# The expert's tokens gathered in quarter rows and turned on VectorE instead of TensorE

## The chip, the cores and the metric

The kernel runs on one core of a Trainium2 chip. The metric is the device time of one execution in microseconds (us), as a median of several runs. The engines are TensorE (PE in the profile, its weight loads PEld), VectorE (DVE), ScalarE (ACT), GpSimd (POOL) and SyncE (SP, which only issues transfers here). SBUF is the memory on the core in which the tiles lie, PSUM the one into which TensorE writes, DRAM the chip's large memory.

## The reference, cut to what matters

```python
# attention: B=8, H=8, S=576, D=64, causal, window 128, a linear bias by distance
x = attention(q, k, v)                      # [4608, 512]
logits = x @ w_gate                         # [4608, 8]
# greedy: the largest logit first; a token goes to one expert, an expert takes 576 tokens
for idx in np.argsort(-logits.flatten()):
    tok, e = idx // 8, idx % 8
    if assigned[tok] >= 0 or counts[e] >= 576: continue
    assigned[tok] = e; counts[e] += 1
for e in range(8):
    mask = assigned == e
    out[mask] = np.maximum(x[mask] @ w1[e], 0) @ w2[e]     # w1 512x1024, w2 1024x512
```

## The kernel before

**Stages.** Attention comes first (to about 220 us of the profile). It writes x to DRAM. Then the router makes the token list of the first expert (to about 242 us), and the rest is eight experts, one after the other, here k = 0 to 7 in the order in which they fill up.

**One expert.** Each fp32 operand of the two layers is split into two parts (`hh`/`xh` the rounded one, `hlo`/`xl` the rest; `hl` holds both parts of a weight), and a product is three matmuls. `layer1` runs over eight blocks f of 128 hidden units: 24 matmuls of 288 tokens each (`ph`, L893). Each f fills two PSUM banks and there are four, so f+2 can begin only when ScalarE (L899) and VectorE (L904) have read the banks of f. `layer2` runs over five tiles t of tokens (four of 128, one of 64, whose two halves are added by L932 and L933), 112 matmuls in all (`po`, L922, L923, L925). After each tile a scatter (an indirect DMA issued by POOL, L934) writes its rows to the places in the output that the list gives; the fifth of expert k is sent when layer 1 of k+1 has already begun.

**Beside the matmuls.** Both layers hand control back often (31 times per expert), and `slot(k, i)` then issues what else there is to do: one step of the router, one weight load (SP) or one split of a loaded weight (`split`: ScalarE's copy and VectorE's two subtractions `hl`, L837). A scheduler then puts the instructions of each engine into a row, and the engine works through this row in order; an instruction whose data isn't there holds up all behind it on its engine. Instructions marked with `keep_in_program_order` keep the order of the code among themselves. Before the change, transfers of the expert stage are not marked.

**The tokens of the next expert.** From step 16 of expert k on, `slot` gathers the tokens of k+1 (`gather`, five indirect DMAs on POOL, L846, each for up to 128 rows of 2 KB, one token per partition) and `turn` brings the 512 features to the partitions: per tile four transposes on TensorE (L870, into the bank `pg`), ScalarE's copy to `xh` (L873), VectorE's subtraction to `xl` (L874). `xh` and `xl` exist once, so their parts for k+1 can be written only when layer 1 of k has read them.

**The router.** `route` (the generator `Router.phase`) makes one list in about 15 steps; `WAITS` says how many slots lie between them. From k=1 on it works one expert further ahead, so that during expert k the list of k+2 is made. The steps touched here: `place` and `indicate` (`kq`, `ind`, L545, L555), `count` (nine matmuls, L579), `enough` (`odd`, `junk`, `sat`, L587 to L593, on VectorE, and a small matmul of `sat`, L596, whose result `narrow` uses for a new bound `lo`, L646); then the update of the table L1 of logits on POOL (L764, L759, L765), from which the next list begins; and from each chosen token's rank the list itself: the rank is divided by 64 slots, one-hot tables `loOH` (L736), `hOH` and `mv` are made on VectorE, and 18 matmuls of 40 columns (L741) turn them into `idx`, 128 partitions by five tiles. Constants come with one DMA at the start (`craw`).

```python
WAITS = (2, 1, 3, 1, 1, 2, 3)
...
        if i >= 16 and k + 1 in r.idx:
            if k not in gathers:
                gathers[k], st["turn"] = m.turn(m.gather(r.idx[k + 1])), i + TURN_WAIT
            elif i >= st["turn"]:
                next(gathers[k], None)
```

## Time and profile before

| | us |
|---|---|
| median of 3 runs | 715.52 (715.28 to 719.58) |
| the profiled execution, its own time | 715.13 |
| its span in the profile | 713.4 |
| attention | to about 220 |
| eight experts | about 242 to 713 |
| one expert in the steady part | 58 |
| PE / DVE / ACT / POOL busy over the span | 679.1 / 466.0 / 331.1 / 154.5 |

The page of a profile gives the busy time of each engine, the span in 40 slices (a digit is the busy share in tenths; `PEclk` is the clock that TensorE was granted), the groups of instructions by line, and the chain of waits that ended last. A row of the timeline has start, duration, engine, line, operation, output and input, and in square brackets how long the engine was idle before and what ended that. A row of the windows has busy time of each engine, with the count of instructions, then TensorE's clock, the share of the DMA engines and GB/s. The profiled execution took 1.7 us more than its span.

### The profile page before, as it was taken

The numbers are of one execution on the slowest core, as the hardware profiler recorded it, in microseconds if no ns is written. First come the engines' busy times: TensorE is split into PE (matmuls) and PEld (weight loads), VectorE is DVE, ScalarE is ACT, GpSimd is POOL, SyncE is SP. The second block draws the span as 40 slices with busy tenths as digits, with TensorE's granted clock in tenths as the row PEclk, the third lists the DMA queues.
The fourth block names the chain that finished last, engine by engine and source line by source line (L and its number), as shares of the span: only waits on it lengthen the run. The fifth ranks groups of instructions, "written<-read, shape, count | busy, mean of one in ns | idle before, by whom it ended". The sixth has DMA issues, their size and how long they took to land.

```text
span 713.4 us, 19210 instructions
## 1 busy us (share of the span) xinstructions
PE 679.1 (95%) x7447; PEld 596.6 (84%) x7447; DVE 466.0 (65%) x1855; ACT 331.1 (46%) x991; POOL 154.5 (22%) x337
## 2 busy tenths in 40 slices
PE   7999999999995699999999999999999999999996
PEld 4898888888874399789889889988988988988985
DVE  6778777877887789869578828846765724523210
ACT  6888888888873253324233223314324324322210
POOL 4121221221220301533042132132033023011011
PEclk9999999999997699999999999999999999999998
DMA  8465465465522352718135235135134334301001
GB/s 301 137 212 181 145 215 181 154 211 177 163 85 61 115 190 89 238 44 272 47 122 205 84 109 177 47 117 177 60 119 131 122 104 137 131 30 37 1 24 49
DMA packets 35140, 92.74 MB, mean 130 GB/s; under 512 B 3808, under 2 KB 13152, under 8 KB 35040
## 3 DMA queue, kind: packets, MB, share of 16 engines
q1 hardware_dynamic: 29152, 72.55, 31.0%
q0 software_dynamic: 5888, 18.88, 8.1%
q8 instruction: 61, 1.00, 0.6%
q14 instruction: 39, 0.32, 0.1%
HBM read 72.54 MB, written 18.87 MB: 128 GB/s over the span
## 4 chain that ended last, share of the span: by engine, by line
PE 76%; DVE 13%; DMA 4%; issue 4%; POOL 1%; SPq 1%; ACT 0%; POOLq 0%; DVEq 0%
PE ph L893 27%; PE po L922 10%; PE po L923 10%; PE po L925 8%; DVE u L133 6%; PE s L53 5%; PE pt L53 4%; PE pt L157 4%; PE x L53 3%; PE pg L870 2%; DVE xb L255 2%; PE m L579 1%; DMA craw<-in_cst_dram 1%; DVE PT L165 1%; DMA g<-x,idx 1%
## 5 line engine op out<-in xcount | busy, mean ns | idle before, releaser
L893 PE MATMUL ph<-xh,hl 128*128 128x288 f32 (+2 forms) x1024 | 192.0, 299 | 0.0
L893 PEld LDWEIGHTS ph<-xh,hl 128*128 128x128 f32 x1024 | 154.6, 189 | 1.0
L144 ACT ACTIVATE u<-u,mn 128x192 f32<-128x192 f32 (+2 forms) x288 | 123.8, 433 | 22.5 <-DVE mn L133 22.5
L922 PE MATMUL po<-hl,hh 128*128 128x512 f32 (+1 forms) x328 | 130.7, 399 | 0.0
L923 PE MATMUL po<-hl,hh 128*128 128x512 f32 (+1 forms) x328 | 126.4, 385 | 0.0
L893 PE MATMUL ph<-xl,hl 128*128 128x288 f32 (+2 forms) x512 | 115.9, 297 | 0.0
L899 ACT ACTIVATE hh<-ph 128x288 fp32r<-128x288 f32 (+2 forms) x128 | 46.6, 409 | 147.5 <-PE ph L893 141.4
L133 DVE CUSTOM_DVE_ANT_0 u<-s,bm 128x192 f32<-128x192 f32 x308 | 86.4, 333 | 39.5 <-PE s L53 39.0
L925 PE MATMUL po<-hl,hlo 128*128 128x512 f32 (+1 forms) x264 | 101.7, 385 | 0.0
L837 DVE TENSOR_TENSOR hl<-raw,hl 128x512 fp32r<-128x512 f32 x128 | 85.0, 683 | 14.4 <-ACT hl L835 13.9
L934 POOL DMA_INDIRECT out_dram<-o,idx x40 | 44.1, 1104 | 204.3 <-ACT o L929 120.9
L893 PEld LDWEIGHTS ph<-xl,hl 128*128 128x128 f32 x512 | 84.2, 189 | 0.1
L874 DVE TENSOR_TENSOR xl<-pg,xh 128x512 fp32r<-128x512 f32 (+1 forms) x37 | 23.7, 639 | 85.6 <-ACT xh L873 84.6
L904 DVE SCALAR_TENSOR_TENSOR hlo<-ph,hh 128x288 fp32r<-128x288 f32 (+2 forms) x128 | 49.5, 416 | 40.0 <-ACT hh L899 38.8
L835 ACT CAST hl<-raw 128x1024 fp32r<-128x1024 f32 x64 | 65.4, 1048 | 15.7 <-DMA raw<-in_w_dram 8.8
L53 PE MATMUL s<-qk 64*64 64x192 f32 (+1 forms) x1112 | 69.1, 319 | 2.0 <-DVE mn L133 1.7
L922 PEld LDWEIGHTS po<-hl,hh 128*128 128x128 f32 x328 | 61.7, 188 | 11.1
L923 PEld LDWEIGHTS po<-hl,hh 128*128 128x128 f32 x328 | 61.8, 188 | 10.7
L929 ACT COPY o<-po 128x512 f32<-128x512 f32 (+1 forms) x33 | 18.9, 574 | 96.1 <-PE po L925 62.1
L846 POOL DMA_INDIRECT g<-x,idx x40 | 45.1, 1126 | 81.9 <-PE pg L870 33.8
L157 PE MATMUL pt<-ident_sb,u 128*128 128x128 f32 x368 | 53.8, 281 | 7.3 <-DVE PT L165 6.0
L925 PEld LDWEIGHTS po<-hl,hlo 128*128 128x128 f32 x264 | 49.6, 188 | 10.3
(217 smaller groups left out, 931.9 us busy)
## 6 DMA issues: line engine op xcount, KB each, us to landing
raw<-in_w_dram SPq DMA_DIRECT2D x64, 512.0 KB, 4.3
qk<-in_qk_dram SPq DMA_DIRECT2D x32, 576.0 KB, 5.0
v<-in_v_dram SPq DMA_DIRECT2D x32, 288.0 KB, 3.8
x<-xb SPq DMA_DIRECT2D x14, 512.0 KB, 3.5
x<-xb SPq DMA_DIRECT2D x8, 128.0 KB, 2.6
x<-xb SPq DMA_DIRECT2D x4, 256.0 KB, 3.4
g<-x,idx POOLq DMA_INDIRECT x40
out_dram<-o,idx POOLq DMA_INDIRECT x40
```

The source lines that it names most:

```text
L53: put(nc.tensor.matmul(out, w, a, start=start, stop=stop, skip_group_check=True))
L133: put(nc.vector.tensor_tensor_reduce(out=u[rows], in0=x[rows, c:c + 64 * m].rearrange("q (j k) -> q j k", k=64), in1=bm[n % NP][rows, y:y ...
L144: put(nc.scalar.activation(u, u, AF.Exp, bias=st["mn"][:, i:i + 1], scale=-1.0, accum_out=st["sm"][:, i:i + 1]))
L157: put(nc.tensor.transpose(ps[:, c:c + 128], u[:, o + 128 * j:o + 128 * j + 128], ident))
L835: self.last = nc.scalar.copy(hl[:, 0, :], raw)
L837: nc.vector.tensor_tensor(hl[:, 1, c:c + 512], raw[:, c:c + 512], hl[:, 0, c:c + 512].bitcast(F32), ALU.subtract)
L893: nc.tensor.matmul(pp[t], w[:, a, j, fo:fo + 128], x[:, j, cut[t]:cut[t + 1]], start=(j == 0 and a == 0 and x is xh), stop=(j == 3 and a = ...
L899: nc.scalar.activation(o, pp[t], AF.Relu)
L904: nc.vector.scalar_tensor_tensor(d, pp[t][:, c0:c1], 0.0, o[:, c0:c1].bitcast(F32), ALU.max, ALU.subtract)
L922: nc.tensor.matmul(out, a, wh, start=(f == 0), stop=False)
L923: nc.tensor.matmul(out, a, wl, start=False, stop=(f == 7 and t == 4))
L925: nc.tensor.matmul(out, hl[:, f, 128 * t:128 * t + 128], wh, start=False, stop=(f == 7))
```

## The change

From the third expert on (k+1 from 2 on):

- `gather_quarters` takes the place of `gather`: 18 indirect DMAs on POOL, each of 128 quarter rows of 512 bytes. A group of 32 tokens lies on 32 partitions for each of the four quarters, so that a tile of 128 tokens is four such DMAs. It needs an index list `gi` of 128 by 18, made with the token list. It is issued in `slot` from step 2 on, not 16.
- `turn_quarters` takes the place of `turn`: VectorE transposes blocks of 32 by 32 within a tile (one instruction per tile, into `tr` in SBUF, two buffers), in place of four TensorE transposes; `xh` and `xl` are made from `tr`. It is issued from step 16 on, as before.
- The features then lie in another order on the partitions, so w1 is laid out for that on the host, and the TensorE transposes of the first two experts read every fourth element.

In the router, for every list but the first: the rank is divided by 32 slots, 9 matmuls of 160 columns take the place of 18 of 40, four copies and one f32 matmul (`r32`) bring the list to all four groups of partitions, `loOH` is half as big and `hOH` and `mv` twice, and `WAITS` is shorter (one step more, about five slots less per list). The constants grow from 611 to 750 columns. All gathers and scatters of the expert stage are marked with `keep_in_program_order` (`self.put`).

```diff
-WAITS = (2, 1, 3, 1, 1, 2, 3)
+WAITS = (1, 1, 2, 1, 1, 1, 2, 1)
+QUARTERS = 2
...
+            loOH = los[:, 0:NT * 32].rearrange("p (c s o) -> p c s o", s=16, o=2)
...
+            yield WAITS[6]
+            ip = self.bank()
+            for c in range(0, NT, 4):
+                nc.tensor.matmul(ip[:, 0:160], loOH[:, c:c + 4].rearrange("p c s o -> p (c s o)"),
+                                 mv[:, c:c + 4].rearrange("p c a h -> p (c a h)"), start=(c == 0), stop=(c == NT - 4))
+            io = self.small("iq", 40)
+            for i in range(4):
+                nc.vector.tensor_copy(io[32 * i:32 * i + 32, :], ip[32 * i:32 * i + 32, 40 * i:40 * i + 40])
+            yield WAITS[7]
+            iq = self.bank()
+            nc.tensor.matmul(iq[:, 0:40], self.C["r32"], io, start=True, stop=True)
+            tk = self.small("tk", 20)
+            nc.vector.tensor_copy(tk, iq[:, 20:40])
+            nc.vector.scalar_tensor_tensor(tk, iq[:, 0:20], 128.0, tk, ALU.mult, ALU.add)
+            gi = self.gi[k] = rs.tile([128, 18], I32, name="gi", bufs=3)
+            nc.vector.tensor_scalar(gi, tk[:, 0:18], 4.0, self.C["quad"][:, 0:1], ALU.mult, ALU.add)
...
+    def gather_quarters(self, gi):
...
+        xq = self.x.rearrange("n (q c) -> (n q) c", q=4)
...
+        for h in range(5):
+            nb = 4 if h < 4 else 2
+            g = self.p["g"].tile([128, DM], F32, name="g")
+            for i in range(nb):
+                self.put(nc.gpsimd.indirect_dma_start(out=g[:, 128 * i:128 * i + 128], out_offset=None, in_=xq,
+                                                      in_offset=bass.IndirectOffsetOnAxis(ap=gi[:, 4 * h + i:4 * h + i + 1], axis=0)))
...
+    def turn_quarters(self, gs):
...
+        for h, (g, nb) in enumerate(gs):
+            r = 32 * nb
+            t = self.p["tr"].tile([128, 4, 128], F32, name="tr")
+            nc.vector.transpose(t[:, :, :r].rearrange("p j (b t) -> p b j t", t=32),
+                                g[:, 0:128 * nb].rearrange("p (b c j) -> p b j c", j=4, c=32))
+            nc.scalar.copy(xh[:, :, 128 * h:128 * h + r], t[:, :, :r])
+            nc.vector.tensor_tensor(xl[:, :, 128 * h:128 * h + r], t[:, :, :r], xh[:, :, 128 * h:128 * h + r].bitcast(F32), ALU.subtract)
+            yield
...
-                put(nc.tensor.transpose(ps[:, j, :r], g[:r, 128 * j:128 * j + 128], self.C["ident"][:r, :r]))
+                put(nc.tensor.transpose(ps[:, j, :r], g[:r, :].rearrange("t (c j) -> t j c", j=4)[:, j], self.C["ident"][:r, :r]))
...
-            self.sent = nc.gpsimd.indirect_dma_start(out=self.out, out_offset=bass.IndirectOffsetOnAxis(ap=idx[:r, t:t + 1], axis=0),
-                                              in_=o[:r, :], in_offset=None)
+            self.sent = self.put(nc.gpsimd.indirect_dma_start(out=self.out, in_=o[:r, :], in_offset=None,
+                                                              out_offset=bass.IndirectOffsetOnAxis(ap=idx[:r, t:t + 1], axis=0)))
...
-CONSTS = [("onef", 128, F32), ("e8", 8, F32), ("jj", 64, F32), ("pcol", 1, F32), ("ids", NT, F32),
-          ("ones", 128, BF), ("tri", 128, BF), ("i64", 64, BF), ("h10", 10, BF), ("eb", 8, NT), ("cc", NT, 10)]
+CONSTS = [("onef", 128, F32), ("e8", 8, F32), ("jj", 64, F32), ("pcol", 1, F32), ("ids", NT, F32), ("quad", 1, F32), ("r32", 128, F32),
+          ("ones", 128, BF), ("tri", 128, BF), ("i64", 64, BF), ("h20", 20, BF), ("eb", 8, NT), ("cc", NT, 10)]
...
+        if k + 1 >= QUARTERS and i >= 2 and k + 1 in r.gi and k not in gathers:
+            gathers[k], st["turn"] = m.turn_quarters(m.gather_quarters(r.gi[k + 1])), 16
```

POOL's row in the program around one expert, before: `Lt` and the two `L` are the update of L1, `out_dram` a scatter, `g` a gather.

```order
L764 TENSOR_SCALAR Lt<-T_7051 128x288
L759 TENSOR_TENSOR L_7219<-L_72,pen 128x288
L765 TENSOR_TENSOR L_72<-Lt,L_7219 128x288
L934 DMA out_dram<-o,idx 4608x512
L846 DMA g<-x,idx 128x512 x2
L934 DMA out_dram<-o,idx 4608x512
L846 DMA g<-x,idx 128x512
L934 DMA out_dram<-o,idx 4608x512
L846 DMA g<-x,idx 128x512
L846 DMA g<-x,idx 64x512
L934 DMA out_dram<-o,idx 4608x512 x2
```

The same place after the change (with the line numbers of the changed kernel):

```order
L1005 DMA out_dram<-o,idx 4608x512 x5
L902 DMA g<-x,gi 128x128 x18
L804 TENSOR_SCALAR Lt<-T_7024 128x288
L799 TENSOR_TENSOR L_7192<-L_72,pen 128x288
L805 TENSOR_TENSOR L_72<-Lt,L_7192 128x288
```

Before, the gathers stood between the scatters of layer 2, behind the update of L1; now 18 of them stand behind all five scatters of the expert before and ahead of that update.

VectorE's row in layer 1 of the fourth expert (k=3), before: `ind` belongs to the router's second counting step, `hh` and `hlo` read layer 1's banks, `odd`, `junk` and `sat` belong to `enough`.

```order
L555 TENSOR_TENSOR ind_7457<-kq_7455,c_i64_425 128x1152 x2
L904 SCALAR_TENSOR_TENSOR hh_7401<-ph_7461,hh_7401 128x64
L643 TENSOR_SCALAR rw_7640<-rw_7531 128x1
L837 TENSOR_TENSOR hl_8029<-raw_7968,hl_8029 128x512
L587 TENSOR_TENSOR odd_7536<-m_7511,pen_7216 64x8
L837 TENSOR_TENSOR hl_8029<-raw_7968,hl_8029 128x512
L590 ISA junk_7539,mx_7538<-m_7511,odd_7536 64x8
L590 ISA mx_7538 64x1
L904 SCALAR_TENSOR_TENSOR hlo_7402<-ph_7497,hh_7401 128x288
L593 TENSOR_SCALAR sat_7541<-mx_7538 64x1
L904 SCALAR_TENSOR_TENSOR hlo_7402<-ph_7498,hh_7401 128x224
```

The same place after:

```order
L556 TENSOR_TENSOR ind_7460<-kq_7458,c_i64_425 128x1152 x2
L975 SCALAR_TENSOR_TENSOR hh_7404<-ph_7464,hh_7404 128x64
L644 TENSOR_SCALAR rw_7629<-rw_7543 128x1
L916 STREAM_TRANSPOSE tr_7955<-g_7483 128x4x4x32
L588 TENSOR_TENSOR odd_7548<-m_7523,pen_7189 64x8
L916 STREAM_TRANSPOSE tr_7980<-g_7488 128x4x4x32
L591 ISA junk_7551,mx_7550<-m_7523,odd_7548 64x8
L591 ISA mx_7550 64x1
L975 SCALAR_TENSOR_TENSOR hlo_7405<-ph_7555,hh_7404 128x288
L594 TENSOR_SCALAR sat_7553<-mx_7550 64x1
L975 SCALAR_TENSOR_TENSOR hlo_7405<-ph_7556,hh_7404 128x224
```

Where two subtractions of a weight stood, the transposes of the first two tiles now stand, ahead of `junk`, `sat` and the `hlo` of the third pair of banks; the subtractions moved further down. The same two transposes stand at that place in the third and fifth experts; in the second, sixth and seventh they stand elsewhere in layer 1.

TensorE's row in layer 2 of an expert, before, from the last of the 18 matmuls of the list on (`m` is the router's bank):

```order
L741 LDWEIGHTS loOH
L741 MATMUL m<-mv,loOH 128x40
L870 MATMUL pg<-ident_sb,g 128x128 x4
L922 MATMUL po<-hl,hh 128x512
L923 MATMUL po<-hl,hh 128x512
L925 MATMUL po<-hl,hlo 128x512
```

After, from the last of the nine on (`iq` holds the four copies, `craw` the constants):

```order
L776 MATMUL m<-mv,loOH 128x160
L993 MATMUL po<-hl,hh 128x512
L994 MATMUL po<-hl,hh 128x512
L996 MATMUL po<-hl,hlo 128x512
L993 MATMUL po<-hl,hh 128x512
L994 MATMUL po<-hl,hh 128x512
L783 MATMUL m<-iq,craw 128x40
L996 MATMUL po<-hl,hlo 128x512
```

The groups of four transposes are gone from the rest of layer 2, and one matmul that needs the four copies has come, five products behind the nine.

More of the change, by code (lines that the diff above doesn't have):

```diff
@@ L723, in phase @@
         slo = rt.tile([128, NT, 2], BF, name="slo")
-        nc.vector.scalar_tensor_tensor(slo, bc(hi.unsqueeze(2), [128, NT, 2]), -64.0, bc(sp[:, 0:NT].unsqueeze(2), [128, NT, 2]),
-                                       ALU.mult, ALU.add)
-        mv = rt.tile([128, NT, 2, 10], BF, name="mv", bufs=1)
-        hOH = hOH.rearrange("p c h o -> p c (h o)")
-        if k == 0:
+        idx = rs.tile([128, 5], I32, name="idx", bufs=4)
+        hOHs, mvs, los = (rt.tile([128, NT * w], BF, name=n, bufs=1) for n, w in (("hOH", 20), ("mv", 40), ("loOH", 64)))
@@ new lines, in slots, with rest @@
+        def slots(w):
+            nc.vector.tensor_scalar(hi, sp[:, 0:NT], 1.0 / w, -(w - 1.0) / (2 * w), ALU.mult, ALU.add)
+            nc.vector.tensor_scalar(hi, hi, MAGIC, MAGIC, ALU.add, ALU.subtract)
+            nc.vector.scalar_tensor_tensor(hv, bc(hi.unsqueeze(2), [128, NT, 2]), 1.0, bc(m.unsqueeze(2), [128, NT, 2]), ALU.add, ALU.mult)
+        def rest(w):
+            nc.vector.scalar_tensor_tensor(slo, bc(hi.unsqueeze(2), [128, NT, 2]), -float(w), bc(sp[:, 0:NT].unsqueeze(2), [128, NT, 2]),
+                                           ALU.mult, ALU.add)
@@ L738, in phase @@
-        yield WAITS[6]
-        ip = self.bank()
-        for c in range(0, NT, 2):
-            self.last_pe = nc.tensor.matmul(ip[:, 0:40], loOH[:, c:c + 2].rearrange("p c s o -> p (c s o)"),
-                             mv[:, c:c + 2].rearrange("p c a h -> p (c a h)"), start=(c == 0), stop=(c == NT - 2))
-        io = rt.tile([64, 20], F32, name="io")
-        nc.vector.tensor_copy(io, ip[64:128, 20:40])
-        ia = rt.tile([64, 2, 5, 2], F32, name="ia")
-        nc.vector.tensor_tensor(ia.rearrange("p a h o -> p (a h o)"), ip[0:64, 0:20], io, ALU.add)
@@ L747, in phase @@
-        idx = rs.tile([128, 5], I32, name="idx", bufs=4)
-        for o in range(2):
-            self.last = nc.vector.scalar_tensor_tensor(idx[64 * o:64 * o + 64, :], ia[:, 0, :, o], 128.0, ia[:, 1, :, o],
-                                                       ALU.mult, ALU.add)
+            loOH = los.rearrange("p (c s o) -> p c s o", s=32, o=2)
+            for a, z in ((0, 24), (24, NT)):
+                nc.vector.tensor_tensor(loOH[:, a:z], bc(self.C["i64"].rearrange("p (s o) -> p s o", o=2).unsqueeze(1), [128, z - a, 32, 2]),
+                                        bc(slo[:, a:z].unsqueeze(2), [128, z - a, 32, 2]), ALU.is_equal)
@@ new lines, in phase @@
+            yield WAITS[6]
+            ip = self.bank()
+            for c in range(0, NT, 2):
+                self.last_pe = nc.tensor.matmul(ip[:, 0:40], loOH[:, c:c + 2].rearrange("p c s o -> p (c s o)"),
+                                                mv[:, c:c + 2].rearrange("p c a h -> p (c a h)"), start=(c == 0), stop=(c == NT - 2))
+            io = rt.tile([64, 20], F32, name="io")
+            nc.vector.tensor_copy(io, ip[64:128, 20:40])
+            ia = rt.tile([64, 2, 5, 2], F32, name="ia")
@@ L811, in start @@
     def start(self, exact):
-        self.ei, self.idx = {}, {}
+        self.ei, self.idx, self.gi = {}, {}, {}
         for _ in self.phase(0, exact):
```

62 lines of the change are left out of this document (44 added, 18 removed).

## The prediction

> **What bounds the kernel now.** I read the page's busy times and slices first, then windows of one expert each, then the chain of waits inside such a window. Experts are counted from k=0 below.
>
> ```profile
> span 713.4 us, 19210 instructions
> PE 679.1 (95%) x7447; PEld 596.6 (84%) x7447; DVE 466.0 (65%) x1855; ACT 331.1 (46%) x991; POOL 154.5 (22%) x337
> PE   7999999999995699999999999999999999999996
> 374.00:432.00 58.00, 57.95 (x407) 51.13 (x406) 38.35 (x122) 18.19 (x34) 15.18 (x16) 1.00 0.38 130
> 432.00:490.00 58.00, 57.99 (x408) 51.30 (x407) 38.47 (x122) 18.27 (x34) 12.90 (x13) 1.00 0.35 114
> by line: PE ph L893 46.0%; PE po L922 16.3%; PE po L923 15.8%; PE po L925 12.7%; PE pg L870 3.8%; PE m L579 3.2%; PE m L741 0.8%; PE m L515 0.7%; PE m L596 0.5%; PE m L693 0.2%; PE m L508 0.2%; issue 0.1%; PE m L713 0.1%; PE m L714 0.0%
> ```
>
> The two window rows are k=2 and k=3: the busy times of PE, PEld, DVE, ACT and POOL, then the granted clock. TensorE is busy 57.95 and 57.99 of 58 us at clock 1.00, so its work is the time here, and what is taken off it is saved unless something new makes it wait. VectorE has 58 − 38.4 = 19.6 us free per expert, POOL over 40. The last row is the chain of 374 to 432 us by line: 3.8% of 58 us, **2.2 us**, are the 20 transposes of L870; 0.8%, 0.46 us, are the 18 matmuls of L741.
>
> **TensorE's own work.** Four transposes in the middle of layer 2, and the rate of layer 1:
>
> ```profile
> 414.63 0.60 PE L870 MATMUL pg<-ident_sb,g 128*128 128x128 f32 x4
> 655.17 25.58 PE ph L893 x192
> ```
>
> The four overlap with their neighbours (0.60 us from first start to last end); the chain gives what they add, 2.2 us for five such groups, 0.44 each. Six experts lose their groups (the third to the eighth): −6 × 2.2 = **−13.2 us**. 192 products of 288 columns take 25.58 us, 0.133 us each. A list by 32 slots has nine products of 160 columns, by columns 9 × 0.133 × 160/288 = 0.67, in place of 0.46; its f32 product with 40 columns (r32) is not in the trace: between one product of the old list (0.46/18 = 0.03) and one 288-column row (0.133), I take 0.12. Seven lists: 7 × 0.33 = **+2.3 us**. The transposes of the first two experts read every fourth element: nothing if they run at the present rate, 2 × 2.2 = 4.4 more if they take twice as long; nothing excludes a small gain, and I take 0, the row of the same operation.
>
> The r32 product waits for four copies of the nine products' result and stands only five layer-2 products behind them, 5 × 0.236 = 1.18 us (L922: 16.3% of 58 us for 40). A small copy, and the handover to TensorE from the rows of sat further down (443.45 to 443.89):
>
> ```profile
> 435.94 0.14 DVE L517 COPY ev<-m 128x1 f32<-128x1 f32 x1
> ```
>
> 4 × 0.14 + 0.44 + a handover from TensorE of about 0.2 (an estimate) = 1.2, as long as the cover; with one hl subtraction (0.68) ahead, 0.7 late. Between 0 and 0.7 I take 0.2 a list: **+1.4**.
>
> **Constants.** They stand on the chain of the start:
>
> ```profile
> 11.53 8.42 DMA craw<-in_cst_dram
> craw<-in_cst_dram SPq DMA_DIRECT2D x1, 305.5 KB
> ```
>
> 305.5 KB become 305.5 × 750/611 = 375 KB; if it is latency it costs 0, if bytes 8.42 × 139/611 = 1.9; I take **+0.5**. So 715.13 (the profiled execution, 0.4 below the median) − 13.2 + 2.3 + 1.4 + 0.5 = **706.1 us if nothing waits for a gather**.
>
> **VectorE's work.** It takes over five 32-by-32 block transposes per expert. The trace has none. A pass over the same 128x512 tile is the nearest row:
>
> ```profile
> L874 DVE TENSOR_TENSOR xl<-pg,xh 128x512 fp32r<-128x512 f32 x29 | 20.0, 689 | 69.3 <-ACT xh L873 69.2
> L736 DVE TENSOR_TENSOR loOH<-c_i,slo 128x2304 bf16<-128x2304 bf16 x7 | 9.4, 1346 | 0.0
> L837 DVE TENSOR_TENSOR hl<-raw,hl 128x512 fp32r<-128x512 f32 x124 | 82.3, 683 | 14.2 <-ACT hl L835 13.7
> ```
>
> 0.69 us each, 4.5 × 0.69 = 3.1 us per expert. The loOH row (1.35 us) halves; hOH and mv double and ten small instructions come. VectorE's 19.6 us per expert cover all of that as work. If a transpose took three times a pass it would still be 9.3 us of 19.6. So its *amount* costs 0; its *place* does not.
>
> **The new wait.** In program order POOL now issues the previous expert's five scatters, then 18 gathers, then the router's L1 update. In k=2, 3 and 4 the scheduler has put the transposes of tiles 0 and 1 into VectorE's row in the middle of layer 1, ahead of `odd`, `junk` and `sat` of the second counting step and of the hlo parts of f=2. Tile 0 needs gathers 1 to 4, tile 1 gathers 5 to 8. When do those land? For k=3, layer 1 starts at 431.22:
>
> ```profile
> 431.22 0.42 PE L893 MATMUL ph<-xh,hl 128*128 128x288 f32 x2
> 433.98 2.03 POOL L934 DMA_INDIRECT out_dram<-o,idx  x1 [3.95 <-DVE em L510]
> 332.86 0.95 POOL L846 DMA_INDIRECT g<-x,idx  x1 [0.30 <-issue]
> 334.11 0.95 POOL L846 DMA_INDIRECT g<-x,idx  x1 [0.30 <-issue]
> L846 POOL DMA_INDIRECT g<-x,idx x40: 912/965/3265, 242.4 to 598.0; - x40
> 594.19 0.97 POOL L846 DMA_INDIRECT g<-x,idx  x1 [0.86 <-PE pg L870]
> 595.40:595.90 0.50, 0.00 (x0) 1.00 0.23 41
> 595.90:596.50 0.60, 0.00 (x0) 1.00 0.77 143
> 596.50:597.20 0.70, 0.00 (x0) 1.00 0.55 222
> 597.20:598.00 0.80, 0.00 (x0) 1.00 0.00 0
> ```
>
> POOL sends the scatter of the last tile at 433.98 for 2.03 us. After 0.30 us between instructions the first gather can begin at 436.3. What does one cost? The source row: minimum 0.912 (64 rows of 2 KB), median 0.965 (128 rows). Half the rows saves 0.05, so nearly all of it is per instruction, and a gather of 128 quarter rows should cost about what one of 128 whole rows does: 0.965 + 0.30 = **1.265 us apart**, as at 332.86 and 334.11. (Were it per byte, 0.24 + 0.30 = 0.54; the 64-row minimum speaks against that.) The last four rows give, for a lone gather issued at 594.19, POOL busy, clock, share of the DMA engines and GB/s: its bytes move until about 597.2, **3.0 us** after the issue began. The eighth gather starts at 436.3 + 7 × 1.265 = 445.2, is there at 448.2, and tile 1 is turned at 448.9. Before:
>
> ```profile
> 441.92 0.17 DVE L587 TENSOR_TENSOR odd<-m,pen 64x8 f32<-64x8 f32 x1
> 443.31 0.14 DVE L593 TENSOR_SCALAR sat<-mx 64x1 bf16<-64x1 f32 x1
> 443.89 0.17 PE L596 MATMUL m<-sat,c_ones 64*128 64x1 bf16 x1
> ```
>
> `odd` stood at 441.92 and sat's product was at 443.89 in TensorE's row, with layer-1 products behind it. After tile 1 come junk, one hlo part and sat, some 0.8 us: TensorE goes on at 449.7, **5.8 us late**, in each of k=2, 3, 4 (17.4 us). At 0.54 apart it would be 445.2 − 0.73 × 7 = 440.1, so about 0.7 us late; at 1.9 apart about 10.
>
> The other experts go the same way, with other instructions behind the transposes:
>
> ```profile
> 601.61 25.58 PE ph L893 x192
> 604.22 1.12 POOL L934 DMA_INDIRECT out_dram<-o,idx  x1 [3.96 <-DVE o L933]
> ```
>
> For k=6 (layer 1 from 601.61) they stand ahead of hlo of f=2, whose banks f=4 needs 4 × 24 × 0.133 = 12.8 us after layer 1's start; the last scatter ends at 3.7 there (4.8 at k=3), so tile 1 is done at 448.9 − 431.2 − 1.1 = 16.6, plus 0.8: 4.6 us late. For k=5 they stand ahead of hlo of f=3, which f=5 needs at 16.0: 17.7 + 0.8 − 16.0 = 2.5. For k=1 the order has `gi` itself in layer 1, ahead of them; if the gathers begin 10 us in (an estimate from that place), tile 1 ends near 24, and the hlo of f=4 behind it is needed at 6 × 24 × 0.133 = 19.2: between 0 and 6, I take 4. Sum: 17.4 + 4.6 + 2.5 + 4 = **28.5 us**. The last three tiles are turned in layer 2, when all gathers have landed.
>
> A stall has a second price in the clock:
>
> ```profile
> 222.00:224.00 2.00, 0.03 (x1) 1.00 0.37 113
> 224.00:226.00 2.00, 0.21 (x4) 0.63 0.40 121
> 226.00:228.00 2.00, 0.41 (x5) 0.50 0.36 94
> 240.00:242.00 2.00, 2.00 (x22) 0.50 0.79 315
> 242.00:244.00 2.00, 2.00 (x6) 0.50 0.01 4
> 244.00:246.00 2.00, 2.00 (x9) 0.75 0.46 131
> 246.00:248.00 2.00, 1.91 (x11) 1.00 0.69 168
> 225.79 0.44 PE L446 MATMUL m<-OH,ind 128*128 128x16 bf16 x5 [3.76 <-DVE ind L446]
> ```
>
> At 225.79 TensorE had been idle for 3.76 us, and the granted clock fell to 0.63 and 0.50. In continuous work from 240 on it stayed at 0.50 to 244, and 1.00 was back by 246: at half speed for about 4 us of work, which loses 2. For the four stalls over 3.76 us (k=2, 3, 4, 6) I take 1.5 each, **+6**; nothing if the idle time comes in shorter pieces. [...]
>
> Sum: 706.1 + 28.5 + 6 = 740.6, **741 us**. Bounds: all six stalls shorter by 2 us and no clock loss give 722.6; 2 us longer each and the full 2 us of clock give 754.6, with the strided transposes 759.
>
> **Rivals.** *A, the gathers land in time.* If POOL needs a quarter of the time for a quarter of the bytes and the issue hides, no instruction waits: 706.1, between 704 and 709 by the terms above. For it: every gather in the trace moves rows of 2 KB, so none shows what a smaller row saves. Against: the 64-row minimum of 0.912, and 3.0 us to landing. It decides at 0.4 us per gather, where tile 1 is ready by 441.9.
>
> *B, the stalls are small and eat the gain.* At 0.54 to 0.9 us apart, 0.7 to 3.2 us for each of the six without clock loss: 709 to 722, slower or faster by a little. The sign changes at 715.1 − 706.1 = 9 us of stalls in all, about 0.65 apart.
>
> *C, POOL itself is late and the list with it.* Slower than the forecast:
>
> ```profile
> 286.03 3.27 POOL L846 DMA_INDIRECT g<-x,idx  x1 [0.30 <-issue]
> 285.99 2.48 DVE L837 TENSOR_TENSOR hl<-raw,hl 128x512 fp32r<-128x512 f32 x4
> 458.71 0.43 POOL L764 TENSOR_SCALAR Lt<-T 128x288 f32<-128x288 bf16 x1 [22.69 <-DVE T L688]
> ```
>
> The gather at 286.03 took 3.27 us in place of 0.96, beside four hl subtractions on VectorE (285.99 to 288.47). At 1.9 + 0.3 apart 18 gathers take 40 us, from 436.3 to 476: the L1 update, 458.71 now, would be 17 us later, VectorE's row halts at the next reduction of L1, and the next list's first steps with it: 17 us less the 5.8 already lost, some 10 us for each of four experts on top of the forecast: 770 to 780 with all four, above 759 with two. It decides where the 18 end after VectorE reaches that reduction, about 1.6 apart. [...] C gets little for another reason: while VectorE waits for a gather it makes no subtraction, and the gathers at 332.86 and 334.11 show 0.95 again.
>
> **Chances.** Forecast (722 to 759, its own range) 0.64; A 0.16 (704 to 709); B 0.12 (709 to 722); C 0.08 (above 759). The range 706 to 759 leaves out most of C and about half of A. One per cent (7.2 us) is about what a measurement tells from no change: below 708.4 lies nearly all of A, 0.15; from 708.4 to 722.7 the rest and B, 0.13; slower 0.72.
>
> **What would show it.** In the new profile: POOL's 18 gathers in one run about 1.27 apart, starting some 5 us after layer 1; VectorE's first two transposes of k=2 to 4 with idle time ended by the gather's DMA; TensorE idle once per expert, 5 to 6 us, ended by `sat`, with clock digits below 9 behind it; no L870 rows after the second expert. The L1 update later than before but not waited for shows C wrong. I am wrong if a quarter gather takes clearly less than 0.9 us, if the eighth lands by 442, or if TensorE has other work than the waiting product to fill the gap.

## The result, and the profile after

The changed kernel takes **818.3 us** (median of 4 runs, 816.01 to 823.32) against 715.52: ratio **1.143**, 95% interval 1.136 to 1.150. The forecast was 741, range 706 to 759. The same kernel was timed again in two later sessions: 809.8 (before: 714.3) in one, **754.0** (before: 715.2) in the other. That difference is part of the result, and the experiments turn on it.

The page after: span, busy times, the forty slices of TensorE and of its clock, and the group of the gathers.

```profile
span 814.2 us, 19024 instructions
PE 696.2 (86%) x7277; PEld 612.4 (75%) x7278; DVE 492.6 (60%) x1934; ACT 332.7 (41%) x991; POOL 232.0 (28%) x415
PE   7999999999839989659939966996699599689996
PEclk9999999999959999869969997998899789889998
L902 POOL DMA_INDIRECT g<-x,gi x108 | 109.5, 1014 | 40.2 <-issue 32.0
```

TensorE was idle for 34 us of 713; now it is idle for 118 of 814, and its slices show the holes, one or two per expert, with a clock below 9 beside them. Windows of k=2 and k=3, with the columns of the first fence of the prediction:

```profile
395.33:469.15 73.82, 60.11 (x380) 53.29 (x378) 42.29 (x134) 18.61 (x34) 27.27 (x26) 0.88 0.29 91
469.15:543.53 74.38, 59.81 (x379) 53.08 (x378) 42.37 (x134) 18.49 (x34) 27.35 (x26) 0.91 0.28 89
```

k=2 took 58.0 us and takes 73.8: TensorE is idle for 13.7 of them, and its work takes 2.2 longer, at a mean clock of 0.88. The timeline of this expert, POOL, then VectorE, then TensorE. Layer 1 starts at 395.33.

```profile
398.10 2.03 POOL L1005 DMA_INDIRECT out_dram<-o,idx  x1 [3.69 <-DVE em L511]
400.43 1.91 POOL L902 DMA_INDIRECT g<-x,gi  x1 [0.30 <-issue]
...
410.70 0.95 POOL L902 DMA_INDIRECT g<-x,gi  x1 [0.31 <-issue]
...
423.46 0.94 POOL L902 DMA_INDIRECT g<-x,gi  x1 [0.30 <-issue]
...
408.82 1.08 DVE L916 STREAM_TRANSPOSE tr<-g 128x512 f32<-128x512 f32 x1 [3.39 <-DMA g<-x,gi]
413.28 1.08 DVE L916 STREAM_TRANSPOSE tr<-g 128x512 f32<-128x512 f32 x1 [3.18 <-DMA g<-x,gi]
414.86 0.14 DVE L594 TENSOR_SCALAR sat<-mx 64x1 bf16<-64x1 f32 x1
427.16 0.17 DVE L588 TENSOR_TENSOR odd<-m,pen 64x8 f32<-64x8 f32 x1 [7.72 <-remote]
...
415.05 0.18 PE L597 MATMUL m<-sat,c_ones 64*128 64x1 bf16 x1 [6.95 <-DVE sat L594]
419.65 0.49 PE L580 MATMUL m<-OH,ind 128*128 128x16 bf16 x9
428.08 0.18 PE L597 MATMUL m<-sat,c_ones 64*128 64x1 bf16 x1 [6.28 <-DVE sat L594]
```

The first half is the forecast. The last scatter ends 4.8 us into layer 1, the gathers follow 1.25 apart, VectorE's two transposes each end an idle stretch that a gather's DMA ended, and the product of `sat` comes after **6.95 us** of idle TensorE (5.8 were forecast). The second half is not in it. TensorE's nine counting products (L580) run from 419.65 to 420.14, the next instruction on VectorE that reads them, `odd`, starts at 427.16, and the profile calls what released it "remote": something none of its engines accounts for. TensorE meanwhile stands still for another 6.28 us, until the `sat` made from that `odd`.

What came late can be read from the semaphore that TensorE counts up after a product, by setting each recorded count beside the end of the product that makes it:

```
k=2 of the changed kernel: product ends, count arrives (us)
layer 1 (ph)     418.42   420.65
nine of L580     420.14   427.14
layer 1 (ph)     421.80   427.24
end of the last of the 18 gathers' issues: 424.40
```

Two counts that belong 1.66 us apart arrive 0.1 apart, 7.0 and 5.4 us late. In the whole kernel before no count is over 1.2 us late; here 22 are over 2, the latest by 17.95 (in k=1, where one wait is 14.3 us), all of them within a run of 18 gathers. From k=1 to k=6 the last of these arrive 2.7 to 3.1 us behind the end of the last gather's issue; the last packets of that gather end 1.2 to 1.3 us behind it (425.70 in k=2), so the counts still come some 1.4 to 1.9 us after it has landed. Counts of VectorE, ScalarE and POOL are never over 0.4 us late. A caution: the ends of TensorE's products are modelled in the profile, and the lateness is reckoned from them. Here the starts of the next products of layer 1 went on at their pace up to the one that needs `sat` (0.24 us apart at clock 0.50, 0.13 apart from 420.84 on at clock 1.00), so the products weren't slow; what held the counts up isn't shown.

Three groups of waits of the whole kernel after, by engine and line (total, times, longest):

```profile
PE m L597 <- DVE sat L594: 56.3, 8, 14.3
DVE odd L588 <- remote: 35.9, 4, 14.1
DVE tr L916 <- DMA g<-x,gi: 28.6, 9, 4.1
```

VectorE waits 28.6 us for gathers and 35.9 for late counts at `odd` alone. That the 28.6 is close to the forecast's 28.5 is chance: the forecast's figure is time that TensorE loses.

### The profile page after: what moved, and what is told of

The parts are those of the page before. It is cut to its first block, busy times and chain, and to the rows that moved or that the text cites. A ratio compares the mean times of both kernels' runs of the same rounds, so it can differ in the third digit from the quotient of the medians.

```text
span 814.2 us, 19024 instructions
## 1 busy us (share of the span) xinstructions
PE 696.2 (86%) x7277; PEld 612.4 (75%) x7278; DVE 492.6 (60%) x1934; ACT 332.7 (41%) x991; POOL 232.0 (28%) x415
## 4 chain that ended last, share of the span: by engine, by line
PE 55%; DVE 20%; issue 6%; another core or an unknown queue 5%; POOL 5%; DMA 5%; ACT 1%; SPq 0%; DVEq 0%; POOLq 0%; ACTq 0%
PE ph L964 18%; PE po L993 7%; PE po L994 7%; PE po L996 6%; DVE u L133 6%; PE s L53 5%; PE pt L53 4%; PE pt L157 4%; POOL g L902 3%; PE x L53 2%; DVE hl L879 2%; DMA raw<-in_w_dram 2%; DMA g<-x,gi 2%; DVE xb L255 1%
## 5 line engine op out<-in xcount | busy, mean ns | idle before, releaser
L964 PE MATMUL ph<-xh,hl 128*128 128x288 f32 (+2 forms) x1024 | 210.7, 320 | 14.3 <-DVE hlo L975 7.3
L964 PEld LDWEIGHTS ph<-xh,hl 128*128 128x128 f32 x1024 | 170.4, 207 | 18.8 <-issue 9.4
L964 PE MATMUL ph<-xl,hl 128*128 128x288 f32 (+2 forms) x512 | 125.8, 317 | 5.5 <-issue 5.5
L993 PE MATMUL po<-hl,hh 128*128 128x512 f32 (+1 forms) x328 | 127.3, 389 | 0.0
L994 PE MATMUL po<-hl,hh 128*128 128x512 f32 (+1 forms) x328 | 126.4, 385 | 0.0
L902 POOL DMA_INDIRECT g<-x,gi x108 | 109.5, 1014 | 40.2 <-issue 32.0
L964 PEld LDWEIGHTS ph<-xl,hl 128*128 128x128 f32 x512 | 92.6, 207 | 5.6 <-issue 5.5
L144 ACT ACTIVATION_READ_ACCUMULATOR u<-u,mn 128x1 f32 x288 | 54.6, 189 | 0.0
```

The lines of the kernel that those rows point to most:

```text
L144: put(nc.scalar.activation(u, u, AF.Exp, bias=st["mn"][:, i:i + 1], scale=-1.0, accum_out=st["sm"][:, i:i + 1]))
L902: self.put(nc.gpsimd.indirect_dma_start(out=g[:, 128 * i:128 * i + 128], out_offset=None, in_=xq, in_offset=bass.IndirectOffsetOnAxis(ap=g ...
L964: nc.tensor.matmul(pp[t], w[:, a, j, fo:fo + 128], x[:, j, cut[t]:cut[t + 1]], start=(j == 0 and a == 0 and x is xh), stop=(j == 3 and a = ...
L993: nc.tensor.matmul(out, a, wh, start=(f == 0), stop=False)
L994: nc.tensor.matmul(out, a, wl, start=False, stop=(f == 7 and t == 4))
```

## The experiments

Five sessions, each on one chip with its own runs of the kernel before. The last column says how many of TensorE's counts (the expectations call them updates) came over 2 us late in the profiled execution, and how late the latest was.

```
session  kernel       median   before   ratio (95%)               late, latest
first    after        818.3    715.5    1.143 (1.136 to 1.150)    22, 18.0
1        list_only    729.1    715.0    1.017 (1.012 to 1.023)     0
1        turn_put     727.7    715.0    1.016 (1.010 to 1.021)     0
1        probe18      739.5    715.0    1.033 (1.026 to 1.040)     0
1        probe_gap    779.6    715.0    1.089 (1.081 to 1.097)     0
2        put_vec      804.8    716.5    1.123 (1.120 to 1.126)    33, 16.5
2        wait_only    817.6    716.5    1.140 (1.135 to 1.145)    22, 17.2
2        turn_dummy   808.7    716.5    1.128 (1.123 to 1.133)    29, 16.9
2        order_only   716.6    716.5    1.001 (0.999 to 1.003)     0
3        after_2      809.8    714.3    1.133 (1.120 to 1.147)    25, 17.0
3        turn_put_2   803.0    714.3    1.124 (1.117 to 1.131)    31, 16.9
3        put_vec_2    793.8    714.3    1.111 (1.104 to 1.118)    30, 16.9
3        probe18_2    811.5    714.3    1.136 (1.131 to 1.141)    31, 16.9
4        spread       713.0    713.3    0.999 (0.997 to 1.000)     0
4        probe18_3    739.7    713.3    one run                    0
4        probe_gap_2  781.4    713.3    one run                    0
4        probe_plain  718.1    713.3    one run                    0
5        spread3      713.5    715.2    0.998 (0.997 to 1.000)     0
5        after_3      754.0    715.2    1.055 (1.051 to 1.059)     0
```

Letters in the expectations name the theories of their round.

### Session 1: which part costs

**The list alone.** The changed kernel with whole rows for all experts: the new list, its constants and the strided transposes stay, quarter gathers and block transposes go.

```diff
-QUARTERS = 2
+QUARTERS = 8
```

> The changed kernel with whole-row gathers and TensorE transposes for every expert: only the list by 32 slots, the shorter waits, the layout and the program order of transfers are left. No run of more than about seven indirect DMAs is left on POOL. Both theories on the long wait (below) put its cause in the quarter gathers, so both expect the terms of the prediction alone: 715.5 + 2.3 + 1.4 + 0.5 = about 720 us, between 714 and 726. A third theory, that the new list or the program order is what costs, expects 750 or more.

Measured 729.1, 14 us above before and 3 above the expected range. From one expert's first product of layer 1 to the next's, the steady experts (k=2 to 4) take 60.0 us for 58.0, the first expert 3.5 more. Part of the 2.0 is a wait of TensorE in the sort of the list:

```profile
410.35 0.19 PE L714 MATMUL m<-ex,c_ones 128*128 128x36 bf16 x1 [0.83 <-DVE ex L711]
```

It stands there in each steady expert; with the waits between the steps shortened, VectorE is not done with `ex`.

**The transposes out of layer 1.** In program order with the transfers, so that all five stand in layer 2.

```diff
-            nc.vector.transpose(t[:, :, :r]...
+            self.put(nc.vector.transpose(t[:, :, :r]...
```

> The changed kernel with VectorE's transposes kept behind what is traced before them on VectorE, so that none stands in layer 1. Theory V (the whole loss is VectorE waiting for gathers, and what is late behind it is its consequence): 704 to 712 us, TensorE no longer idle in layer 1. Theory H (while POOL sends a long run of indirect DMAs, TensorE's semaphore updates reach the other engines up to 17 us late, whoever reads the gathered data): the 18 gathers are still in a row, so layer 1 still has waits of 7 to 14 us per expert on updates of TensorE, 750 to 800 us in all.

Measured 727.7, in neither theory's range. No wait for a gather is left on VectorE, `odd` follows its products at once, and the L1 update behind the 18 gathers now ends last: rival C, at a price of 3.9 us in k=2, 3 and 4.

```profile
396.27 0.17 DVE L588 TENSOR_TENSOR odd<-m,pen 64x8 f32<-64x8 f32 x1 [0.43 <-PE m L580]
412.65 0.64 DVE L490 TENSOR_REDUCE b<-L 128x36 f32<-128x288 f32 x1 [4.08 <-POOL L L805]
415.49 0.91 PE L776 MATMUL m<-mv,loOH 128*128 128x160 bf16 x9 [3.89 <-DVE mv L769]
```

**The gathers alone.** The kernel before, with 18 unread quarter gathers per expert on POOL in layer 1, once as they are and once with a fill of 128x1024 ahead of each.

```diff
+        if 1 <= k < 7 and i == 2:
+            for n in range(18):
+                tc.keep_in_program_order(m.nc.gpsimd.memset(z, 0.0))     # probe_gap only
+                d = m.p["gd"].tile([128, 128], F32, name="gd")
+                tc.keep_in_program_order(m.nc.gpsimd.indirect_dma_start(
+                    out=d, out_offset=None, in_=x.rearrange("n (q c) -> (n q) c", q=4),
+                    in_offset=bass.IndirectOffsetOnAxis(ap=r.idx[k][:, 0:1], axis=0)))
```

> The kernel of before, unchanged in its work, with 18 more gathers of 128 quarter rows in layer 1 of the second to the seventh expert, in a row behind the previous expert's scatters; nothing reads what they bring. Theory V: no engine waits for them, 715 to 720 us. Theory H: TensorE's updates are late during each run, layer 1 of six experts longer by 5 to 14 us, 745 to 800 us in all.

> As probe18, but with a fill of 128x1024 on POOL ahead of each of the 18 gathers, so that they come some 2.2 us or more apart in place of 1.25. Theory V: 715 to 725 us. Theory H in the form that the rate of issue decides: hardly any update over 1 us late, 715 to 725 us; in the form that the count of gathers decides: as probe18, 745 to 800 us.

739.5 and 779.6, the first in neither theory's range, the second in one for another reason than expected. What they cost is one wait, rival C again: VectorE's first reduction of L1 stands behind the update on POOL.

```profile
342.09 0.64 DVE L489 TENSOR_REDUCE b<-L 128x36 f32<-128x288 f32 x1 [14.01 <-POOL L L765]
```

It is 14.0 us in k=1 and 23.6 in four waits in all; with the fills 56.5 in four waits, the longest 15.3. probe18 is 24.5 us above before and probe_gap 64.6, at a mean clock of 0.973 and 0.955 in the profiled execution (before: 0.975 to 0.985 over its runs in session 1). Beside these waits and the lower clock, no price of 18 gathers in a run shows there. So far everything pointed to the transposes in layer 1 as the sole price, and left 818 unexplained: the late counts were in none of these four traces.

### Session 2: a remedy and two halves of the suspect

All but the last on top of turn_put. put_vec puts the L1 update on VectorE, so that nothing stands behind the gathers. wait_only lets VectorE read four numbers of the gathers of tiles 0 and 1 in layer 1 (the wait, without the transposes there); turn_dummy makes two block transposes of data at hand there (the work, without the wait). order_only is the kernel before with its gathers and scatters in program order.

```diff
-            eng = nc.vector if k == 0 else self.tc.nc.gpsimd        # put_vec
+            eng = nc.vector
...
+                m.put(m.nc.vector.tensor_copy(tiny, st["gs"][h][0][0:1, :]...          # wait_only, h = 0, 1
...
+                m.nc.vector.transpose(t..., st["now"][:, 0, 0:512]...                  # turn_dummy, twice
...
-            nc.gpsimd.indirect_dma_start(out=g[:r, :], ...                             # order_only
+            self.tc.keep_in_program_order(nc.gpsimd.indirect_dma_start(out=g[:r, :], ...
```

> As turn_put (VectorE's transposes out of layer 1), and the router's update of L1 on VectorE in place of POOL, so that it no longer stands behind the 18 gathers. Theory: what is left of turn_put's loss in k=2 to 5 of its profile is the wait for that update, 3.9 us each and TensorE's lower clock after it. If so: about 727.7 - 4 x (3.9 + 1.5) = 706 us, 702 to 712. If the update isn't what is waited for: 725 to 730.

> As turn_put, with two copies of four numbers on VectorE in layer 1, one that reads what gathers 1 to 4 bring and one for 5 to 8, at the place where the changed kernel has its two transposes. Theory W (TensorE's updates are late when VectorE waits for gathers in layer 1, with no transpose needed): updates of TensorE 2 to 17 us late again, layer 1 12 to 16 us longer per expert, 790 to 820 us. Theory S (the block transposes on VectorE during the run of gathers cause the lateness): only the first wait of some 7 us per expert and its clock, no update more than 1 us late, 760 to 780 us.

> As turn_put, with two more block transposes on VectorE in layer 1, of tokens that lie in SBUF already, so that VectorE transposes during the run of gathers but waits for none of them. Theory S: updates of TensorE 2 to 17 us late, 760 to 800 us. Theory W: none late, VectorE's 2 x 1.1 us more per expert hidden, 726 to 735 us.

> The kernel of before with nothing but its gathers and scatters kept in the order of the code. In list_only, which has this, the list by 32 slots and the strided transposes together, an expert in the steady part took 60 us in place of 58. If the program order of transfers costs that: 722 to 730 us. If the list does: 714 to 718 us.

Program order costs nothing: 716.6 for 716.5. The other three came out at 805, 818 and 809, all far above turn_put's 728, put_vec too, which takes a wait away. All three have late counts; put_vec should have been near 706. Either each of the three edits had a hidden price of 80 us, or the session had. The next runs decide that.

### Session 3: the same kernels again

No edit: after, turn_put, put_vec and probe18, in another session.

> The changed kernel itself, beside turn_put, put_vec and probe18 on one chip in one session: in the first session (list_only, turn_put, probe18, probe_gap) no update of TensorE came over 0.5 us late, in the second (put_vec, wait_only, turn_dummy) and in the first profile of the changed kernel up to 17 us. Theory K (the kernel decides): here too turn_put and probe18 show none late and the others do: after_2 about 818 us. Theory M (the machine or session decides, and the gathers bring it out): either all four show late updates, or none; where none does, after_2 is 740 to 750 us, the prediction's two stalls and the list's 14 us.

> Theory K: 728 us again, no update late. Theory M: the same as the other three, 780 to 810 us where updates are late, 728 where none is.

> Theory K: 805 us again, updates late. Theory M: as turn_put_2; where no update is late, 702 to 712 us, the wait for the L1 update gone.

> The kernel of before with 18 unread gathers per expert. Theory K: 739.5 us, none late. Theory M: late updates here too where the session has them, 760 us or more.

turn_put went from 728 to **803**, probe18 from 739.5 to **811**, with no change in the code, while the kernel before stayed at 714. k=2 of turn_put_2, TensorE's counting products and what VectorE does with them:

```profile
410.24 0.44 PE L580 MATMUL m<-OH,ind 128*128 128x16 bf16 x9
414.53 0.17 DVE L588 TENSOR_TENSOR odd<-m,pen 64x8 f32<-64x8 f32 x1 [4.08 <-remote]
421.60 0.22 DVE L647 SCALAR_TENSOR_TENSOR lo<-w,m,low 128x1 f32<-128x1 f32 x1 [5.60 <-remote]
```

The first `odd` comes 3.8 us behind the end of its product, `lo` 5.6 us after VectorE ran idle, both released by "remote"; in turn_put the same `odd` waited 0.43, for the product. That the lateness belongs to a kernel's code fell here: it belongs to a condition that held in the first measurement and in sessions 2 and 3, and it strikes kernels with long runs of indirect gathers, whoever reads them. probe18_2 says most, as nobody reads its gathers and nothing but the run of 18 was added. Within session 3, put_vec_2 is 9.2 us below turn_put_2. That isn't rival C's wait removed: in turn_put_2 none of VectorE's reductions of L1 waits for the update on POOL (14.1 us in turn_put). What differs is the waits for late counts at `odd` and `lo` that "remote" ended, 49.8 us in turn_put_2 and 33.6 in put_vec_2, so no run shows what put_vec is worth without late counts.

### Session 4: other runs of transfers

spread is turn_put with the gathers in five groups of at most four, each released by a copy of its index columns on VectorE (`go`) at slots 2, 6, 10, 14 and 17. probe_plain replaces the 18 gathers of probe18 by plain transfers of the same size; probe_gap and probe18 are repeated.

```diff
+        with self.tc.issue_after(self.seen.ins):                    # spread
+            nc.vector.tensor_copy(go[:, 0:nb], gi[:, 4 * h:4 * h + nb])
...
+            if len(gs) < 5 and i >= (2, 6, 10, 14, 17)[len(gs)] and st.get("last") != (k, i):
+                gs.append(m.gather_tile(r.gi[k + 1], len(gs)))
...
-                tc.keep_in_program_order(m.nc.gpsimd.indirect_dma_start(...            # probe_plain
+                tc.keep_in_program_order(m.nc.gpsimd.dma_start(
+                    d, x.rearrange("n (q c) -> (n q) c", q=4)[128 * n:128 * n + 128]))
```

> As turn_put, but the 18 gathers go out in five groups of four (the last of two), each released by a copy of its indices on VectorE behind the hlo of a block of layer 1 (f=0, 2, 4, 6 and the start of layer 2), so that no more than four follow each other and the L1 update on POOL comes between. Theory G (where updates of TensorE are late at all, lateness grows with the run of gathers issued back to back, from the fourth or fifth on): hardly any update over 2 us late, 703 to 722 us either way. Theory T (any 18 gathers in layer 1 do it, however spread): 760 us or more where updates are late.

> The kernel of before with 18 unread gathers per expert, as the mark of whether updates are late at all beside the other three: 811 us with updates up to 17 us late, or 739 us with none.

> The kernel of before with 18 unread gathers and a fill on POOL ahead of each, so that they come some 2.6 us apart. Theory G, if the rate decides: no update over 2 us late even where probe18_3 has them; the time about 780 us as the first time, from the L1 update alone. If the count decides: updates late by 5 us or more, 800 us or more.

> The kernel of before with 18 plain transfers of the same size (128 rows of 512 bytes) issued by POOL in place of the unread gathers. If a long run of transfers that POOL issues is enough: updates as late as in probe18_3. If it takes the indirect form: none late, 715 to 745 us.

probe18_3 is 739.7 with no late count: session 4 was one without late counts, so it can't say whether shorter runs, gaps or plain transfers avoid the lateness; that stays inconclusive. It shows two other things. A plain transfer costs POOL 0.54 us where a gather of the same bytes costs 0.95 and 0.30 of pause:

```profile
316.19 8.05 POOL L1038 DMA_DIRECT2D gd<-x  x15
```

And spread takes both waits of the change away from the third expert on. Its k=2, and VectorE's wait in k=1:

```profile
381.81:438.37 56.56, 56.15 (x379) 49.81 (x378) 43.04 (x139) 18.27 (x34) 28.14 (x26) 1.00 0.36 117
358.01 0.64 DVE L490 TENSOR_REDUCE b<-L 128x36 f32<-128x288 f32 x1 [2.79 <-POOL L L805]
```

56.6 us for 58.0, and TensorE idle for 0.4 of them. k=2 to k=6 together gain 9 us. But the first expert takes 5.2 more and k=1 3.7 more, of which 2.8 is this wait for the L1 update, so that 713.0 against 713.3 is no difference.

### Session 5: the best version, and the changed kernel a third time

spread3 is spread with `QUARTERS = 3`: the first three lists stay as they were before, and one more expert gathers whole rows. after_3 is the changed kernel itself.

```diff
-QUARTERS = 2
+QUARTERS = 3
...
-        if k == 0:
+        if k < QUARTERS:
             slots(64)
```

> As spread, with quarter gathers from the fourth expert on in place of the third, and the list by 64 slots for the first three: in spread the third to seventh expert took 1.4 to 2.6 us less than before, 9 us in all, and the first two 9 us more. If the loss there comes from their lists by 32 slots and the early quarter gathers: 703 to 709 us. If it comes from the strided transposes of the first two experts, which stay: 710 to 714. If long runs alone make updates of TensorE late, neither it nor spread shows any, also where after_3 does; if spread runs make them late too, 740 us or more there.

> The changed kernel beside it. Where no update of TensorE is late, the prediction's own mechanism is left alone: turn_put's 728 us plus one wait of VectorE of 6 to 7 us and its lower clock in each of four or five experts, 750 to 770 us. Where updates are late, 806 to 823 us as twice before.

spread3 takes 713.5 against 715.2, ratio 0.998 (0.997 to 1.000): again not to be told from before. Its k=1 falls from spread's 63.7 to 61.9, without the wait for the L1 update. Its first expert still takes 3.7 us more than before, though its first three lists are made by 64 slots as before: what the first expert loses isn't the list by 32 slots. The time lies where the expectation put it if the strided transposes cost it; the shorter waits between the router's steps, which spread3 has too, would look the same. The first product of layer 1 lies at 251.4 where it lay at 249.75; that place varies between 249.0 and 253.2 over these traces. No version was found that beats the kernel before by more than a measurement tells.

after_3 is the run that settles the forecast: **754.0**, no late count. Its page, k=2, and the rows that answer to those of the first profile:

```profile
PE 681.3 (91%) x7277; PEld 599.5 (80%) x7278; DVE 492.1 (66%) x1934; ACT 331.7 (44%) x991; POOL 237.1 (32%) x415
379.58:445.75 66.17, 58.71 (x380) 51.94 (x378) 42.40 (x134) 18.39 (x34) 27.96 (x26) 0.92 0.32 100
393.08 1.08 DVE L916 STREAM_TRANSPOSE tr<-g 128x512 f32<-128x512 f32 x1 [3.41 <-DMA g<-x,gi]
397.55 1.08 DVE L916 STREAM_TRANSPOSE tr<-g 128x512 f32<-128x512 f32 x1 [3.19 <-DMA g<-x,gi]
404.45 0.17 DVE L588 TENSOR_TENSOR odd<-m,pen 64x8 f32<-64x8 f32 x1 [1.07 <-PE m L580]
399.32 0.18 PE L597 MATMUL m<-sat,c_ones 64*128 64x1 bf16 x1 [6.97 <-DVE sat L594]
```

The same instructions, the same two waits for gathers, the same idle time of 6.97 us ahead of `sat`, and then `odd` 1.07 us after VectorE ran idle, released by its own product: no second hole. The eight experts take 564.9 us in the first profile and 500.7 here. So **64 us** of the change's 103 go with the late counts (TensorE is idle for 118.0 us there and for 69.5 here, and its work takes 14.9 us longer there, at a mean clock of 0.928 for 0.963), and 37 to 39 are what the forecast was about.

## Why the prediction was wrong, and where it was right

**The step that failed** is the sum of the waits, 28.5 us and 6 of clock: it lets TensorE go on as soon as the gather has landed, the tile is turned and `sat` is made, one hole per expert, and holds no term for TensorE's results being announced late while the gathers run. In the first measurement there were two holes in k=2 to k=4, and the late counts stand for 64 us. None of the rivals had them either; C, which stood above 759, names another mechanism, and VectorE doesn't wait for the L1 update at all in the profile after.

The rest can be held against after_3, whose 754.0 lies in the forecast's own range (722 to 759). It is 13 above the forecast's 741, and that it lies inside is partly luck: the transposes saved 2.2 us more than forecast, while the waits took 3 us more, the clock 6 and the first expert 3.4. Lengths in us, each against before; the seven lists stand where the trace has their products, two in k=1 and none in k=6. The measured transposes and lists come from spread, the waits and the clock from after_3 against spread, and all are rounded:

```
              transposes, lists, wait, clock
              forecast                            measured in after_3
first expert       +0.5              = +0.5                              +3.9
k=1           -2.2 +1.1 +4.0         = +2.9                              +2.2
k=2           -2.2 +0.5 +5.8 +1.5    = +5.6       -2.6 +1.2 +7.0 +2.6    +8.1
k=3           -2.2 +0.5 +5.8 +1.5    = +5.6       -2.6 +1.2 +7.1 +2.0    +7.7
k=4           -2.2 +0.5 +5.8 +1.5    = +5.6       -2.6 +1.2 +7.0 +1.7    +7.3
k=5           -2.2 +0.5 +2.5         = +0.8       -2.6 +0.6 +3.0 +2.9    +3.9
k=6           -2.2      +4.6 +1.5    = +3.9       -2.6      +4.7 +2.6    +4.8
last                                    0                                -0.9
```

- **The wait, its place and its cause: right.** 7.0, 7.1 and 7.0 us in k=2 to 4 (5.8 forecast), 3.0 in k=5 (2.5), 4.7 in k=6 (4.6), 2.8 in two pieces in k=1 (4). turn_put moves the transposes out of layer 1 and changes nothing else; in session 1 none of these waits is left in it, and it takes 727.7. The pace was 1.25 (1.265), the run began 5.1 us into layer 1 (5.1). What made it some 1.2 longer in k=2: the first and third gather took 1.91 and 1.45, so that the eighth started 15.4 us into layer 1 and not 14.0; it was usable 2.6 us later, not 3.0; and the second transpose took 0.4 more than the pass of 0.69 that stood in for it:

```profile
L916 DVE STREAM_TRANSPOSE tr<-g 128x512 f32<-128x512 f32 x24 | 25.8, 1086 | 33.0 <-DMA g<-x,gi 30.6 <-issue 2.4
```

  1.09 us where a pass over the tile is 0.69. As work it costs nothing, as forecast: VectorE is busy for 42.4 of 66.2 us.
- **The clock: right in kind, too small.** Windows behind the hole of after_3 that ended at 399.3 (TensorE's busy time, granted clock, DMA share, GB/s):

```profile
399.30:401.30 2.00, 1.98 (x9) 0.50 0.14 37
401.30:403.30 2.00, 2.00 (x17) 0.50 0.22 61
403.30:405.30 2.00, 2.00 (x17) 0.58 0.13 37
405.30:407.30 2.00, 2.00 (x16) 1.00 0.13 33
```

  Half speed for some 5.7 us. spread does the same TensorE work without a hole: 56.15 us busy at clock 1.00 against 58.71, so the hole's second price is **2.6 us** in k=2. Reckoned the same way it is 2.0 and 1.7 in k=3 and 4, 2.9 and 2.6 in k=5 and 6. The forecast took 1.5 for four of them, an estimate below the 2 us that it read from its own rows, and nothing for k=5, where 3.0 us of idle time went with 2.9 us of longer work too.
- **The transposes of L870: right in kind, somewhat too small.** In k=6 no list is made, and the transposes are all that spread takes from before:

```profile
601.45:655.01 53.56, 53.56 (x325) 48.41 (x324) 21.65 (x48) 17.67 (x33) 5.02 (x5) 1.00 0.25 82
603.99:654.98 50.99, 50.99 (x305) 46.60 (x304) 26.01 (x58) 17.86 (x33) 23.24 (x23) 1.00 0.34 109
```

  2.6 us for the 2.2 that were forecast. Transposes that read every fourth element, for which 0 was taken, cost 0.3 us more per expert: k=6 of list_only, which has them and no list either, takes 53.9.
- **The list: about right in k=5, more in the steady experts, and not what the first expert loses.** 0.33 + 0.2 us were taken. With the transposes' 2.6 set aside, spread pays 0.6 in k=5 and 1.2 in k=2 to 4, of which 0.4 is idle time. list_only's 2.0 is no measure of it, since its transposes are the slower ones there; 0.83 of it is the wait for `ex`, which is 0.33 in k=2 of after_3. The 0.2 for a handover from TensorE rests on no row; in the trace of before VectorE starts 0.04 us behind the end of a product that it waits for (median of 74 waits, the longest 0.18). In the first expert 0.5 was taken and 3.5 to 3.9 measured in list_only, turn_put and after_3; spread3 loses 3.7 there without a list by 32 slots. TensorE is busy for 2.3 us more there in after_3 and idle for 1.5 more. Whether the shorter waits between the router's steps, which bring work forward, or the slower transposes do it, no run separates.
- **Rival C: small, and waiting behind.** With the transposes out of the way (turn_put) it cost 3.9 us in each of three experts. Its condition in the forecast, gathers 1.6 apart, was wrong: at 1.25 (the median in turn_put) it already bites once nothing else waits first.
- **Program order and constants: no price seen.** 716.6 for 716.5 in order_only; the first product of layer 1 moved by 0.3 in after_3 (0.5 taken), inside its own spread.

## What to carry to other kernels

Cutting a gather into smaller rows multiplied its price here, which is by the instruction (0.95 us on POOL for 128 quarter rows, 0.965 for 128 whole ones): 18 at 1.25 us made an engine with 20 us to spare hold up the one with none, because the reader's place in its row came before the data. Price such an edit at the place in the row that waits, and release the transfers in short groups from where there is room: spread had no such wait left from the third expert on, though only sessions without late counts tried it, and its gain was eaten by the first two experts. And time a change in more than one session before explaining it: the same kernel took 728 and 803 us, and the kernel before told nothing of the difference.

## What the hardware showed that was not expected

**TensorE's counts come late during long runs of indirect DMAs, in some sessions.** Three sessions of six had it, in every kernel with 18 gathers in a run (eight traces, 22 to 33 counts over 2 us late, the latest 16.5 to 18.0), and in none of the traces of the other three. The kernel before is at 713 to 716.5 throughout, and who reads the gathers, or whether anybody does, doesn't change whether counts come late. The last late counts of a run arrive some 2 to 3.5 us behind the end of its last issue in all eight traces, in most of them two or more within 0.15 us. Shorter runs show a little of it: in order_only, in session 2, counts come up to 1.9 us late during runs of five gathers, and cost no time (716.6 for 716.5). The trace of before holds a small one too: during seven indirect DMAs from 369.57 on, ScalarE waits for products that ended at 376.63, and gets going at 377.46.

```profile
376.09 1.89 POOL L846 DMA_INDIRECT g<-x,idx  x1 [0.30 <-issue]
377.46 0.71 ACT L899 ACTIVATE hh<-ph 128x288 fp32r<-128x288 f32 x2 [2.92 <-PE m L515]
```

**What stays open.** What makes a session one with late counts is not known; sessions 1 and 2, a quarter of an hour apart, name the same chip number, one without and one with (whether it was the same machine isn't recorded). One thing went with it each time: the traces of the other three sessions hold 15.9 to 16 landing events per indirect DMA, and the eight traces with late counts some 7 on average over all indirect DMAs of the kernel, and only 3 to 4 within the runs of 18. That of order_only, with its small lateness, holds 13.1, the trace of before 14.5. Every timed execution here comes with a recorded span and clock. Whether the lateness is a price of recording and not of the kernel no run shows, since none was timed without a recording; nor does one show whether the missing events and the late counts have one cause. Nor was spread run under the condition, so that runs of four escape it is a guess, from before and order_only, whose runs of at most seven show no count over 2 us late.
